# A routed feed-forward on one core: the first expert in plain float32, and the second stage's gating moved from VectorE to ScalarE and GpSimd

## The chip, the core and the metric

The kernel runs on one core of a Trainium2 chip. A core has engines that work side by side, each through its own instructions in order: TensorE (PE in the profile; its weight loads are PEld), VectorE (DVE), ScalarE (ACT), GpSimd (POOL) and SyncE (SP), which here issues transfers. They share an on-chip memory (SBUF); TensorE writes to PSUM. An instruction that needs another engine's result waits at the head of its engine's queue, and all behind it wait too. The metric is the time of one execution on the device in microseconds.

## What is computed

Attention gives 2304 tokens of 512 numbers. Each of 8 experts takes 288 of them, by a greedy choice over all scores in falling order, and sends them through its own two-matrix network. A second, common network with a gate follows. Cut to what matters:

```python
# expert e, for its 288 tokens (mask)
h = np.maximum(x[mask] @ w1[e], 0.0)      # 512 -> 1024
out[mask] = h @ w2[e]                     # 1024 -> 512
# second network, for all tokens
h = x @ w_in                              # 512 -> 2048
relu6 = np.clip(h + 3.0, 0.0, 6.0)
g = h * relu6 / 6.0
return g @ w_out                          # 2048 -> 512
```

## The kernel before

After attention (to about 300 us of the trace) the work goes by **slots**, one an expert, in the order in which experts fill up. A slot holds one expert's 288 tokens, transposed, and has 24 **steps**: 8 of the first stage (`kind` 0, the expert's network, 128 hidden units a step) and 16 of the second (`kind` 1, the gated network). A step is `l1` (4 blocks of 128 into the hidden units `h`, a PSUM tile with 2 buffers), the activation `ev` (for `kind` 1 the gating), and `l2` (into 4 accumulators `acc`). `l2` of a step is issued after `l1` of two steps later (`LAG = 2`), so that the activation has that long.

The matmuls are in a rounded float32 format, fp32r. To keep precision every operand is split into a high part (a rounded copy, `xh`, `yh`, `gh`, the first half of `w`) and a low part (the difference, `xl`, `yl`, `gl`), and each product is made of three: high by high, high by low, low by high (L1118 to L1120 in `mm3`, L1187 to L1190 in `l1`). A step has 24 matmuls of 288 columns. Weights are split by `split_w` (L1106 on ScalarE, L1108 the low part, on GpSimd; in slot 0 every sixth on VectorE). The second network's weights are the same for all slots: they are split once in slot 0, half are kept in `WB`, half written to DRAM (`hl`) and read back later. A helper, `Convert`, makes those weights from bits on VectorE (L978 to L981) and a sign multiply on GpSimd (L988), partly within slot 0 (`cv.rest`).

The second stage's gating is: ScalarE `t` = relu(h + 3) (L1204), ScalarE `pc` = h (L1205), VectorE `t` = min(t, 6) x pc (L1206), ScalarE `gh` = t/6 (L1207), VectorE `gl` = t/6 - gh (L1208).

The **router** runs beside this: phase s + 1 finds, during slot s, the next expert's tokens. Its parts, in order: take out the tokens chosen (`close`, `best`), turn the keys (`rx`, `rw`: matmuls of TensorE; copies `ks` by ScalarE; from phase 2 on through DRAM, `kd`, into `rHw` and `rLw`), then a **search** for the 288th largest key: 4 rounds over high digits (`rHw`) and 4 over low (`rLw`). A round counts, in each of 128 partitions, which of 2304 keys reach that partition's threshold. Of the columns VectorE counts 1440 (L714) and ScalarE 864 with a Sign that sums (L716); L717 merges both into `cnt`; a transpose (L722) and a comparison (`fl`, L725) give the next thresholds. Then come `rhs` (a matmul to all partitions, `rp<-rhs`), small VectorE operations, `tot` (three tiny matmuls), positions, `roc`, 20 `ua` matmuls, and `ids`, by which GpSimd gathers the tokens (`xg`). They are transposed on TensorE and split (`x_in`: L1138 and L1139 on ScalarE, L1140 `xl` on VectorE) in the last steps of the slot.

What runs where in an engine's queue comes from the order in which the code is written, then a scheduler's: the router is a generator, and `step()` takes its next unit when a counter (`hold`) that falls by `RATE` a half step reaches zero; every `yield n` puts n onto it, in the search `SLACK` a round.

```python
def step():
    hold[0] -= RATE[s > 0]
    while hold[0] <= 0:
        hold[0] += next(units, 1e9)
```

Of the kernel before, what the change touches and what calls it, by code (L numbers as in the profile page):

```python
# [514 lines left out]
class Router:  # L515
# [288 lines left out]
    def phase(self, s):  # L804
# [6 lines left out]
        if s < E - 1:  # L811
# [13 lines left out]
            half = SHARE  # L825
# [187 lines left out]
def experts(ctx, tc, rt, x_dram, cv, w1, w2, out, ident, cap, B, S):  # L1013
# [52 lines left out]
    def load(s, j):  # L1066

        if j >= FA + FB * (s == 0):
            return
        if j >= FA:  # L1070
            f = j - FA
            raw = raws[s, 1, f] = wp.tile([128, 1024], F32, name="raw", tag="raw", bufs=RAW)
            if f < cv.pre // 2:
                nc.sync.dma_start(raw, cv.wb[:, f])
            else:
                conv.extend([lambda u=u: cv.rest(raw[:, u * 512:(u + 1) * 512], 2 * f + u) for u in range(2)])
# [13 lines left out]
    cnt = [0]  # L1090

    def split_w(i, part):
# [273 lines left out]
```

## Time and profile before

| | |
|---|---|
| median of 3 runs | 1131.04 us (1130.54 to 1137.7) |
| the profiled execution | 1130.45 us, its span in the trace 1128.6 us |
| TensorE busy | 961.0 us (85%), mean granted clock 0.926 |
| VectorE, ScalarE, GpSimd busy | 727.9, 605.6, 435.8 us (64, 54, 39%) |
| slot 0 starts, ends | 346.7, 466.2 us |
| slots 1 to 7 end | 567.8, 668.4, 767.5, 866.6, 959.3, 1038.7, 1128.6 us |

Slot boundaries are the first `l1` matmul of a slot in the trace. The shares of busy time are means over stages with different limits, so what follows is read by slot. A line of a timeline gives start, duration, engine, source line, operation, the tiles written and read, and in brackets how long its engine had been idle before and who released it. The granted clock is a share of TensorE's full speed (1.00 is 2.4 GHz, 0.50 is 1.2 GHz).

### The profile page before, as it was taken

What the parts mean: (1) busy time and instruction counts of PE and PEld (TensorE: products, weight loads), DVE (VectorE), ACT (ScalarE), POOL (GpSimd) and SP (SyncE); (2) the same over time, 40 slices, a digit from 0 to 9 for tenths busy, and PEclk for the clock granted to TensorE, in tenths of its full rate; (3) what the DMA queues carried; (4) which work ended last, traced back from release to release, by engine and by line L of the source; (5) the groups of instructions that cost most, each with busy time, mean ns of one, the idle gap of its engine ahead of it and who ended that gap; (6) DMA issues with size and microseconds to landing.
All of it is one profiled execution on the core that took longest, in us unless ns stands there. A gap on an engine that the chain in (4) does not pass through costs nothing.

```text
span 1128.6 us, 20123 instructions
## 1 busy us (share of the span) xinstructions
PE 961.0 (85%) x6748; PEld 885.6 (78%) x6748; DVE 727.9 (64%) x1933; ACT 605.6 (54%) x1499; POOL 435.8 (39%) x346
## 2 busy tenths in 40 slices
PE   4888888898317788789889889899989999999997
PEld 3676766675217688779789788889978999999996
DVE  7888897986773996783973856586385534234332
ACT  5786776875334764534653563455256235445442
POOL 7657556661424664331250044026104402603400
PEclk9999999998657997889999999899899899999999
DMA  7889879887133865349229525823752562572540
GB/s 172 240 239 258 232 205 266 206 228 202 43 99 112 297 214 163 96 146 270 84 73 286 138 75 195 222 82 119 232 148 68 183 202 90 182 243 73 181 159 21
DMA packets 122999, 190.28 MB, mean 169 GB/s; under 512 B 21904, under 2 KB 72464, under 8 KB 122896
## 3 DMA queue, kind: packets, MB, share of 16 engines
q1 hardware_dynamic: 119136, 179.54, 53.2%
q0 software_dynamic: 3072, 9.44, 2.8%
q8 instruction: 54, 0.88, 0.3%
q14 instruction: 49, 0.40, 0.1%
q10 hardware_dynamic: 688, 0.02, 0.0%
HBM read 144.60 MB, written 25.61 MB: 151 GB/s over the span
## 4 chain that ended last, share of the span: by engine, by line
PE 34%; DVE 20%; issue 8%; DMA 5%; ACT 1%; POOL 1%; POOLq 0%; DVEq 0%; ACTq 0%; SPq 0%
DVE rcmp L714 5%; PE h L1187 5%; PE acc L1119 5%; PE h L1188 5%; PE acc L1120 5%; PE h L1190 5%; PE acc L1118 5%; DMA rHw<-kd 4%; PE rp L701 2%; DVE gl L1201 2%; DVE gl L1208 2%; DVE cnt L717 1%; DVE t L1206 1%; DVE fl L725 1%; POOL w L1108 1%
## 5 line engine op out<-in xcount | busy, mean ns | idle before, releaser
L1108 POOL TENSOR_TENSOR w<-raw,w 128x512 fp32r<-128x512 f32 x135 | 180.6, 1352 | 383.5 <-ACT w L1106 291.4
L1119 PE MATMUL acc<-gl,w 128*128 128x288 f32 x512 | 156.7, 312 | 19.3 <-DVE gl L1208 13.0
L1120 PE MATMUL acc<-gh,w 128*128 128x288 f32 x512 | 153.4, 306 | 0.0
L1118 PE MATMUL acc<-gh,w 128*128 128x288 f32 x512 | 139.9, 310 | 13.7 <-ACT gh L1207 13.5
L1206 DVE SCALAR_TENSOR_TENSOR t<-t,pc 128x288 f32<-128x288 f32 x128 | 61.4, 480 | 117.4 <-ACT pc L1205 117.2
L1119 PEld LDWEIGHTS acc<-gl,w 128*128 128x128 f32 x512 | 101.8, 199 | 24.3 <-DVE gl L1208 16.7
L1204 ACT ACTIVATE t<-h,rthree 128x288 f32<-128x288 f32 x128 | 63.5, 496 | 102.8 <-PE h L1190 97.5
L1118 PEld LDWEIGHTS acc<-gh,w 128*128 128x128 f32 x512 | 93.9, 197 | 16.3 <-ACT gh L1207 16.2
L1106 ACT ACTIVATE w<-raw 128x512 fp32r<-128x512 f32 x144 | 89.6, 633 | 28.5 <-PE acc L1120 16.3
L282 ACT ACTIVATE P<-P,mx 128x128 f32<-128x128 f32 (+2 forms) x144 | 83.6, 581 | 37.1 <-DVE mx L267 35.7
L1120 PEld LDWEIGHTS acc<-gh,w 128*128 128x128 f32 x512 | 101.8, 199 | 0.0
L1201 DVE TENSOR_TENSOR gl<-t,gh 128x288 fp32r<-128x288 f32 x64 | 52.7, 824 | 73.6 <-ACT gh L1200 73.6
L1207 ACT ACTIVATE gh<-t 128x288 fp32r<-128x288 f32 x128 | 56.6, 444 | 64.4 <-DVE t L1206 64.4
L1208 DVE SCALAR_TENSOR_TENSOR gl<-t,gh 128x288 fp32r<-128x288 f32 x128 | 66.1, 517 | 29.8 <-ACT gh L1207 28.0
L1187 PE MATMUL h<-yh,w 128*128 128x288 f32 x256 | 74.4, 309 | 6.6 <-ACT pc L1205 6.6
L1119 PE MATMUL acc<-gl,WB 128*128 128x288 f32 x256 | 75.9, 303 | 2.7 <-DVE gl L1208 2.6
L246 PE MATMUL sc<-kh,qs 128*128 128x128 f32 (+3 forms) x128 | 49.7, 399 | 30.9 <-DVE qs L218 12.2
L1187 PE MATMUL h<-xh,w 128*128 128x288 f32 x256 | 75.3, 313 | 0.3 <-ACT gh L1200 0.3
L1120 PE MATMUL acc<-gh,WB 128*128 128x288 f32 x256 | 74.8, 298 | 0.0
L1188 PE MATMUL h<-xh,w 128*128 128x288 f32 x256 | 74.4, 310 | 0.0
L1188 PE MATMUL h<-yh,w 128*128 128x288 f32 x256 | 72.5, 301 | 0.0
L1187 PE MATMUL h<-yh,WB 128*128 128x288 f32 x256 | 71.1, 298 | 0.0
(294 smaller groups left out, 2806.8 us busy)
## 6 DMA issues: line engine op xcount, KB each, us to landing
w<-hl SPq DMA_DIRECT2D x112, 512.0 KB, 5.0
raw<-in_moe_w_dram SPq DMA_DIRECT2D x128, 256.0 KB, 4.3
kh<-knh SPq DMA_DIRECT2D x60, 144.0 KB, 2.6
raw<-in_moe_w_in_dram SPq DMA_DIRECT2D x16, 512.0 KB, 4.0
raw<-in_moe_w_out_dram SPq DMA_DIRECT2D x16, 512.0 KB, 4.6
hl<-w SPq DMA_DIRECT2D x16, 512.0 KB, 6.2
wb<-wf SPq DMA_DIRECT2D x28, 256.0 KB, 2.9
raw<-wb SPq DMA_DIRECT2D x14, 512.0 KB, 5.0
```

The source lines that it names most:

```text
L282: nc.scalar.activation(x[:, :w], x[:, :w], AF.Exp, bias=mx, scale=-1.0, accum_out=col)
L1106: nc.scalar.activation(hi, src, AF.Copy)
L1108: j = (nc.vector if v else nc.gpsimd).tensor_tensor(lo, src, hi.bitcast(F32), op=OP.subtract)
L1118: nc.tensor.matmul(p, ah, bh, start=first, stop=False)
L1119: nc.tensor.matmul(p, ah, bl, start=False, stop=False)
L1120: rt.behind = nc.tensor.matmul(p, al, bh, start=False, stop=last)
L1187: nc.tensor.matmul(p, wk[k][0], x[k][0], start=(k == 0), stop=False)
L1188: nc.tensor.matmul(p, wk[k][1], x[k][0], start=False, stop=False)
L1201: nc.vector.tensor_tensor(gl, t, gh.bitcast(F32), op=OP.subtract)
L1204: nc.scalar.activation(t, p, AF.Relu, bias=rt.three)
L1206: nc.vector.scalar_tensor_tensor(t, t, 6.0, pc, op0=OP.min, op1=OP.mult)
L1208: nc.vector.scalar_tensor_tensor(gl, t, 1.0 / 6.0, gh.bitcast(F32), op0=OP.mult, op1=OP.subtract)
```

## The change

Four edits. (1) **Slot 0 in plain float32**: `l1_whole` and the first branch of `l2` multiply unsplit tokens, hidden units and weights, 4 matmuls each in place of 12, on raw weight tiles (two of 512 columns, 4 buffers each). x and y are copied once, by ScalarE and VectorE in turn; the gate is two ScalarE operations and one of VectorE. The second network's weights are still split in slot 0, for later slots, after their step, all low parts on GpSimd. (2) **Gating of slots 1 to 7**: VectorE's two operations go; ScalarE takes a second relu (6 - relu(3 - h), so that t ends as relu6), GpSimd the product and the low part. The first stage's `gl` and y's low part stay on VectorE. (3) **The low part of x** goes to GpSimd. (4) **The search from phase 1 on** counts all 2304 columns on VectorE; Sign and merge go; the constants that set the pace change with it.

```diff
-SLACK = 2.6
+SLACK = 2.3
@@ search
-            below = wk.tile([128, 1], F32, name="below", bufs=2)
-            nc.scalar.activation(cmp[:, n:].bitcast(BF), W[:, n:], AF.Sign, bias=T, scale=-1.0, accum_out=below)
-            nc.vector.scalar_tensor_tensor(cnt, below, -0.5, cnt, op0=OP.mult, op1=OP.add)
+            if shared:
+                below = wk.tile([128, 1], F32, name="below", bufs=2)
+                nc.scalar.activation(cmp[:, n:].bitcast(BF), W[:, n:], AF.Sign, bias=T, scale=-1.0, accum_out=below)
+                nc.vector.scalar_tensor_tensor(cnt, below, -0.5, cnt, op0=OP.mult, op1=OP.add)
@@ phase (and in it yield 1 -> 2, yield 3 -> 5; in route, 3 -> 4)
-            half = SHARE
+            half = SHARE if s == 0 else 0
@@ experts
-    EVERY, FIRST = 6, 6
-    RATE = 1.4, 0.9
+    RATE = 1.5, 0.95
@@ split_w
-        v = s == 0 and (cnt[0] % EVERY == 0 or cnt[0] <= FIRST)
-        j = (nc.vector if v else nc.gpsimd).tensor_tensor(lo, src, hi.bitcast(F32), op=OP.subtract)
-        if s == 0 and kind == 0:
-            after(tc, j, rt.last if v else rt.fetch)
+        nc.gpsimd.tensor_tensor(lo, src, hi.bitcast(F32), op=OP.subtract)
@@ x_in
+            if s == 0:
+                x = whole("x", f"x{c}", 1)
+                if c % 2:
+                    nc.vector.tensor_copy(x, p[:, :cap])
+                else:
+                    nc.scalar.activation(x, p[:, :cap], AF.Copy)
+                XT[s].append(x)
+                continue
...
-            nc.vector.tensor_tensor(hl[1], t, hl[0].bitcast(F32), op=OP.subtract)
+            nc.gpsimd.tensor_tensor(hl[1], t, hl[0].bitcast(F32), op=OP.subtract)
@@ new
+    def l1_whole(kind, f, x, w, prev=None):
+        p = ps.tile([128, 512], F32, name="h", tag="h", bufs=2)[:, :cap]
+        for k in range(KC):
+            rt.behind = nc.tensor.matmul(p, w[:, k * 128:(k + 1) * 128], x[k], start=(k == 0), stop=(k == KC - 1))
...
+                nc.scalar.activation(t, p, AF.Relu, bias=rt.three)
+                nc.scalar.activation(pc, p, AF.Copy, scale=1.0 / 6.0)
+                nc.vector.scalar_tensor_tensor(g, t, 6.0, pc, op0=OP.min, op1=OP.mult)
@@ l1
-                nc.scalar.activation(t, p, AF.Relu, bias=rt.three)
-                nc.scalar.activation(pc, p, AF.Copy)
-                nc.vector.scalar_tensor_tensor(t, t, 6.0, pc, op0=OP.min, op1=OP.mult)
-                nc.scalar.activation(gh, t, AF.Copy, scale=1.0 / 6.0)
-                nc.vector.scalar_tensor_tensor(gl, t, 1.0 / 6.0, gh.bitcast(F32), op0=OP.mult, op1=OP.subtract)
+                nc.scalar.activation(t, p, AF.Relu, bias=rt.three, scale=-1.0)
+                nc.scalar.activation(pc, p, AF.Copy, scale=1.0 / 6.0)
+                nc.scalar.activation(t, t, AF.Relu, bias=rt.six, scale=-1.0)
+                nc.gpsimd.tensor_tensor(t, t, pc, op=OP.mult)
+                nc.scalar.activation(gh, t, AF.Copy)
+                nc.gpsimd.tensor_tensor(gl, t, gh.bitcast(F32), op=OP.subtract)
@@ l2
+            if not isinstance(g, tuple):
+                rt.behind = nc.tensor.matmul(p[:, :cap], w[:, o * 128:(o + 1) * 128], g, start=first, stop=last)
+                continue
@@ main loop
+        if s == 0:
+            for u in range(2 * kind):
+                split_w(i, u)
+            load(i + RAW)
```

The change moves line numbers: L714, L721, L722, L725 of before are L715, L723, L724, L727 of the changed kernel, L1108 is L1106, L1187 to L1190 are L1221 to L1224, L1118 to L1120 are L1114 to L1116, L701 is L702.

TensorE's order around phase 2's `rhs` matmul (`rp<-rhs`; `h` is of `l1`, `acc` of `l2`). Before, some six steps into slot 1:

```order
L1187 MATMUL h<-xh,w_5880 128x288
L1188 MATMUL h<-xh,w_5880 128x288
L1190 MATMUL h<-xl,w_5880 128x288 x4
L1118 MATMUL acc_5803<-gh,w_5838 128x288
L1119 MATMUL acc_5803<-gl,w_5838 128x288
L1120 MATMUL acc_5803<-gh,w_5838 128x288
L701 MATMUL rp<-rhs,ronef 128x16
L1159 MATMUL ot<-ident,yo 96x128 x4
L1118 MATMUL acc_5804<-gh,w_5838 128x288
```

After, behind the first steps' `l1` of slot 1 and the last `l2` of slot 0 (`g,raw`), ahead of slot 1's first `l2`, two steps into it:

```order
L1222 MATMUL h<-xh,w_5135 128x288
L1224 MATMUL h<-xl,w_5135 128x288 x4
L1251 MATMUL acc_4564<-g,raw_4948 128x288
L1251 MATMUL acc_4565<-g,raw_4948 128x288
L1251 MATMUL acc_4566<-g,raw_4948 128x288
L1251 MATMUL acc_4567<-g,raw_4948 128x288
L1165 MATMUL ot<-ident,yo 96x128
L702 MATMUL rp<-rhs,ronef 128x16
L1114 MATMUL acc_5309<-gh,w_5016 128x288
L1115 MATMUL acc_5309<-gl,w_5016 128x288
L1116 MATMUL acc_5309<-gh,w_5016 128x288
```

It stands about four steps earlier in slot 1.

VectorE's order within phase 2's search. Before, two high rounds, with gating (L1206, L1208), `xl` and merge between:

```order
L714 TENSOR_SCALAR rcmp,cnt<-rHw,T 128x1440
L721 TENSOR_SCALAR rG<-T,rcz 128x1
L1140 TENSOR_TENSOR xl<-t,xh 128x288
L717 SCALAR_TENSOR_TENSOR cnt<-below,cnt 128x1
L722 STREAM_TRANSPOSE rrowH<-cnt 128x32
L725 SCALAR_TENSOR_TENSOR fl,T<-rrowH,rG 128x33
L1208 SCALAR_TENSOR_TENSOR gl<-t,gh 128x288
L714 TENSOR_SCALAR rcmp,cnt<-rHw,T 128x1440
```

After, the last low round and what follows to `rhs`, with a gate of slot 0 (L1212) and a block of weight conversion (L981 to L984) between:

```order
L715 TENSOR_SCALAR rcmp,cnt<-rLw,T 128x2304
L723 TENSOR_SCALAR rG<-T,rcz 128x1
L981 TENSOR_SCALAR raw_4948<-raw 128x512
L724 STREAM_TRANSPOSE rrowL<-cnt 128x32
L1212 SCALAR_TENSOR_TENSOR g<-t,pc 128x288
L982 SCALAR_TENSOR_TENSOR raw_4948<-raw,raw_4948 128x512
L983 TENSOR_SCALAR raw<-raw 128x512
L727 SCALAR_TENSOR_TENSOR fl,T<-rrowL,rrem,rG 128x33
L984 TENSOR_SCALAR raw_4948<-raw 128x512
L854 TENSOR_SCALAR rhs<-rsel,T 128x8
```

The counts are wider, the merges gone, and the gates of slot 0's last steps stand behind counts.

GpSimd's order in a slot's last steps, after (a stretch of slot 1; `w` splits of the next slot's weights, `t` and `gl` the gating, `xl` of the next tokens):

```order
L1242 TENSOR_TENSOR t<-t,pc 128x288
L1106 TENSOR_TENSOR w_7318<-raw_7291,w_7318 128x512
L1244 TENSOR_TENSOR gl<-t,gh 128x288
L1242 TENSOR_TENSOR t<-t,pc 128x288
L1106 TENSOR_TENSOR w_7419<-raw_7303,w_7419 128x512
L1244 TENSOR_TENSOR gl<-t,gh 128x288
L1242 TENSOR_TENSOR t<-t,pc 128x288
L1106 TENSOR_TENSOR w_7422<-raw_7304,w_7422 128x512
L1146 TENSOR_TENSOR xl<-t,xh 128x288
L1244 TENSOR_TENSOR gl<-t,gh 128x288
```

Before, only the `w` splits stood there. In the last six steps of a slot they are 8 splits, 12 gating operations and 4 `xl`.

## Rows read from the trace of the kernel before

**Rows 1.** Slots 0, 2, 4, 5, 6: us, PE, PEld, DVE, ACT, POOL busy, clock, DMA
```profile
core 0 of [0], span 1128.6 us
...
346.70:466.20 119.50, 97.78 (x630) 91.75 (x630) 92.17 (x191) 72.37 (x163) 63.03 (x47) 0.87 0.59 192
...
567.80:668.40 100.60, 89.17 (x635) 86.16 (x634) 64.24 (x154) 48.91 (x118) 26.37 (x22) 0.97 0.52 153
...
767.50:866.60 99.10, 90.53 (x635) 87.07 (x634) 62.57 (x154) 48.22 (x116) 26.61 (x22) 0.95 0.49 153
866.60:959.30 92.70, 90.44 (x649) 90.11 (x649) 39.97 (x102) 39.35 (x97) 27.34 (x22) 0.94 0.46 149
959.30:1038.70 79.40, 79.04 (x603) 78.78 (x602) 28.32 (x53) 39.26 (x97) 26.92 (x22) 1.00 0.53 175
```

**Rows 2.** TensorE's waits in slots 1 to 4: total us, times, longest us
```profile
PE acc L1119 <- DVE gl L1208: 10.5, 13, 2.3
PE acc L1118 <- ACT gh L1207: 8.4, 8, 2.4
PE h L1187 <- ACT pc L1205: 5.9, 4, 2.9
PE rp L701 <- DVE tot L885: 4.4, 2, 2.7
```

**Rows 3.** ScalarE's timeline in phase 3's search: start, duration, work, idle before
```profile
535.44 1.02 ACT L716 ACTIVATE rcmp<-rHw,T 128x864 bf16<-128x864 uint16 x1 [0.94 <-DVE fl L725]
...
536.79 0.48 ACT L1204 ACTIVATE t<-h,rthree 128x288 f32<-128x288 f32 x1
```

**Rows 4.** VectorE's groups by form, whole kernel: busy us, mean ns, idle before
```profile
L1208 DVE SCALAR_TENSOR_TENSOR gl<-t,gh 128x288 fp32r<-128x288 f32 x128 | 66.1, 517 | 29.8 <-ACT gh L1207 28.0 <-PE acc L1120 0.5 <-issue 0.2
...
L978 DVE TENSOR_SCALAR raw<-raw 128x512 int32<-128x512 int32 x4 | 3.5, 889 | 0.0
```

**Rows 5.** VectorE, 457.7 to 494.5 us (busy, mean ns | idle); counts (min/median/max)
```profile
L717 DVE SCALAR_TENSOR_TENSOR cnt<-below,cnt 128x1 f32<-128x1 f32 x8 | 8.4, 1056 | 0.0
...
L1201 DVE TENSOR_TENSOR gl<-t,gh 128x288 fp32r<-128x288 f32 x6 | 2.7, 445 | 0.0
...
L714 DVE TENSOR_SCALAR_CACHE_REDUCE rcmp<-rHw,T x21: 1703/1709/1715, 296.4 to 831.2; 128x1440 uint16<-128x1440 uint16 x21
```

**Rows 6.** Phase 2: timelines of ScalarE, VectorE; router's matmuls (min/median/max, starts)
```profile
446.90 0.70 ACT L757 ACTIVATE ks<-rw 64x288 uint16<-64x288 f32 x2 [1.16 <-PE rw L701]
...
457.71 1.71 DVE L714 TENSOR_SCALAR_CACHE_REDUCE rcmp<-rHw,rT 128x1440 uint16<-128x1440 uint16 x1 [4.62 <-DMA rHw<-kd]
...
L701 PE MATMUL rp<-ua,roc x20: 209/311/312, 508.6 to 511.8; 128*96 128x6 bf16 x20
...
L701 PE MATMUL rp<-rhs,ronef x2: 366/370/374, 494.5 to 494.7; 128*128 128x16 f32 x2
```

**Rows 7.** Subtractions on GpSimd and VectorE by line; TensorE's timeline at a float32 matmul
```profile
L1108 POOL TENSOR_TENSOR w<-raw,w x135: 1252/1295/2658, 339.8 to 1057.9; 128x512 fp32r<-128x512 f32 x135
...
L1108 DVE TENSOR_TENSOR w<-raw,w x9: 678/679/1279, 332.3 to 419.2; 128x512 fp32r<-128x512 f32 x9
...
L204 POOL TENSOR_TENSOR qnl<-qn,qnh x15: 1405/1436/1951, 20.5 to 239.7; 128x576 fp32r<-128x576 f32 x15
...
69.75 0.66 PE L374 MATMUL mem<-MZ,qp 128*128 128x146 f32 x4
70.25 0.96 PE L393 MATMUL zl<-wg,oT 128*128 128x16 f32 x8
```

**Rows 8.** A merge behind a run of GpSimd; all merges' min/median/max
```profile
480.38 5.05 POOL L1108 TENSOR_TENSOR w<-raw,w 128x512 fp32r<-128x512 f32 x4
...
481.05 4.40 DVE L717 SCALAR_TENSOR_TENSOR cnt<-below,cnt 128x1 f32<-128x1 f32 x1
...
L717 DVE SCALAR_TENSOR_TENSOR cnt<-below,cnt x56: 143/159/4404, 294.2 to 848.5; 128x1 f32<-128x1 f32 x56
```

**Rows 9.** Window behind the `ua` products of slot 2, columns as rows 1
```profile
599.10:602.40 3.30, 3.30 (x15) 3.30 (x16) 0.48 (x3) 0.00 (x0) 1.65 (x2) 0.50 1.03 401
```

More of the change, by code (lines that the diff above doesn't have):

```diff
@@ L635, in consts @@
         nc.vector.memset(t("three", [128, 1]), 3.0)
+        nc.vector.memset(t("six", [128, 1]), 6.0)
         t("keyi", [128, NT, E], I32)
@@ L1064, in gather, with load @@
             rt.fetch = i
-    def load(s, j):
-        if j >= FA + FB * (s == 0):
+    def load(j):
+        s, kind, f = order[j]
+        if s and kind:
             return
[L1070 to L1076, printed above, removed]
+        raw = raws[j] = [wp.tile([128, 512], F32, name=f"raw{u}", tag=f"raw{u}", bufs=RAW) for u in range(2)]
+        if kind:
+            for u in range(2):
+                if f < cv.pre // 2:
+                    nc.sync.dma_start(raw[u], cv.wb[:, f, u * 512:(u + 1) * 512])
+                else:
+                    conv.append(lambda u=u: cv.rest(raw[u], 2 * f + u))
             return
-        f = j
         if f == 0:
@@ L1098, in split_w @@
         hi, lo = w[:, :512], w[:, 512:]
-        W[i, part] = hi, lo
+        if s:
+            W[i, part] = hi, lo
         if kind and s:
@@ L1120, in mm3, with whole @@
         rt.behind = nc.tensor.matmul(p, al, bh, start=False, stop=last)
+    def whole(name, tag, bufs):
+        return act.tile([128, cap], F32, name=name, tag=tag + "h", bufs=bufs)
     def parts(name, tag, bufs):
@@ L1171, in out_units, with y_in @@
         return ev, [tr(a) for a in range(3)]
-    def y_in(acc):
+    def y_in(s, acc):
         y = []
         for o, p in enumerate(acc):
+            if s == 0:
+                y.append(whole("y", f"y{o}", 1))
+                if o % 2:
+                    nc.vector.tensor_copy(y[o], p[:, :cap])
+                else:
+                    nc.scalar.activation(y[o], p[:, :cap], AF.Copy)
+                continue
             hl = parts("y", f"y{o}", 1)
@@ L1180, in y_in, with ev @@
         return y
+    def l1_whole(kind, f, x, w, prev=None):
+        p = ps.tile([128, 512], F32, name="h", tag="h", bufs=2)[:, :cap]
+        for k in range(KC):
+            rt.behind = nc.tensor.matmul(p, w[:, k * 128:(k + 1) * 128], x[k], start=(k == 0), stop=(k == KC - 1))
+            if prev is not None:
+                after(tc, rt.behind, prev)
+                prev = None
+        def ev():
+            g = whole("g", "g", LAG + 2)
+            if kind == 0:
+                nc.scalar.activation(g, p, AF.Relu)
+            else:
+                t = act.tile([128, cap], F32, name="t", tag="t", bufs=2)
+                pc = act.tile([128, cap], F32, name="pc", tag="pc", bufs=2)
+                nc.scalar.activation(t, p, AF.Relu, bias=rt.three)
+                nc.scalar.activation(pc, p, AF.Copy, scale=1.0 / 6.0)
+                nc.vector.scalar_tensor_tensor(g, t, 6.0, pc, op0=OP.min, op1=OP.mult)
+            return g
+        return ev
     def l1(kind, f, x, w, prev=None):
@@ L1224, in ahead @@
             while nw[part] < min(i + 2 * SPLIT[0], len(order)):
-                held = [j for j in range(i - part * LAG, nw[part] + 1) if j >= 0 and not (order[j][1] and order[j][2] % 2)]
-                if len(held) > SPLIT[part] or order[nw[part]][0] not in reg or order[nw[part]][:1] + (0, 0) not in raws:
+                held = [j for j in range(max(i - part * LAG, FA + FB), nw[part] + 1)
+                        if not (order[j][1] and order[j][2] % 2)]
+                if len(held) > SPLIT[part] or nw[part] not in raws and not order[nw[part]][1]:
                     break
@@ L1264, in experts @@
             routed(s + 1)
-            for u in range(RAW):
-                load(s + 1, u)
+            for u in range(RAW if s else 0):
+                load(pos[s + 1, 0, u])
             xs = x_in(s + 1)
@@ L1278, in experts @@
             conv.pop(0)()
-        e = l1(kind, f, X[s, 1] if kind else XT[s], W.pop((i, 0)), rt.behind if kind and f == 1 else None)
+        e = (l1 if s else l1_whole)(kind, f, X[s, 1] if kind else XT[s], W.pop((i, 0)) if s else raws[i][0],
+                                    rt.behind if kind and f == 1 else None)
         step()
```

44 lines of the change are left out of this document (21 added, 23 removed).

## The prediction

> **What bounds the kernel now.** I read the windows by slot first [rows 1]. Slot 6, in which no router runs, takes 79.4 us with TensorE busy for 79.0 of them at full clock: that is the floor of 24 steps, 79.4/24 = 3.31 us a step. Slots 2 to 4 have the same matmuls and take 99.1 to 100.6 us, so 20 us a slot stand above the floor (slot 3 takes 99.1 like slot 4). TensorE's waits from slot 1 to slot 4 [rows 2] say where: for VectorE's `gl` and ScalarE's `gh` of the second stage's gating, for the `pc` copy that frees a PSUM buffer, and for the router's small results. The four rows printed are 29 us, 7 a slot, and I count 9 with the view's smaller ones. The rest is the router's own matmuls (20 `ua` products, 508.6 to 511.8, a start-to-end of 3.45 us [rows 6], and about 1.1 us of others) and low clock: the mean granted clock of slot 4 is 0.95, and at half clock half of the time is lost, so 0.05 x 99 = 5 us. One such stretch stands right behind the `ua` products of one slot: 3.3 us at a granted clock of 0.50 [rows 9], the lower of the two levels (1.2 GHz), worth 1.7 us.
>
> Why the gating is late is in ScalarE's timeline [rows 3]: a Sign count of the search waits 0.94 us for VectorE's `fl`, then runs 1.02 us, and everything behind it in ScalarE's order (`t`, `pc`, `gh`) waits as well (the next `t` starts at 536.79). Search and gating hold each other up.
>
> **The change, part by part.** *Search on VectorE alone (phases 1 to 7).* A count of 1440 columns takes 1.71 us and hardly varies [rows 5]. 2304 columns are between 1.71 (if columns cost nothing) and 1.71 x 1.6 = 2.74; I take 2.6 start to start, since the start-up does not grow: +0.9 a round, 8 rounds, **+7.2 us** of VectorE. The merge `cnt<-below` goes: 8.4 us in the search of phase 2 [rows 5], 1.3 of work (8 x the median 0.159 [rows 8]) and 7.1 of standing behind GpSimd: one merge took 4.40 us while a run of four GpSimd subtractions, 5.05 us, was on [rows 8].
>
> *Gating of slots 1 to 7.* VectorE loses two operations a step (`gl` 0.517 us mean [rows 4], `t` like it), 16 us a slot. ScalarE gets one more activation of 0.4 to 0.5 (0.48 in [rows 3]) and loses the Signs, about 1.2 us each with the read of the sum, 8 a phase; its four gating operations are 1.8 us of a 3.3 us step, so it stays free. GpSimd gets two products of 128x288 a step. No such shape is in the trace on that engine. Its nearest rows are 128x512 at 1.295 us and 128x576 at 1.436 [rows 7]: in proportion 0.73, on the line through both 1.295 - 224 x 0.141/64 = 0.80, and 1.295 if size did not matter. I take 0.77, nearest to the two scalings. The chain from the last `h` matmul to `gl` is then 0.5 + 0.4 + 0.5 + 0.77 + 0.44 + 0.77 = 3.4 us against about 2.3; with LAG = 2 the second matmuls have two steps, 6.6 us, so this is hidden, and only the kernel's end pays it: +1 us.
>
> *Low parts of x on GpSimd.* In the last six steps of slots 1 to 6 GpSimd holds, by the order, 8 weight splits, 12 gating operations and 4 `xl`: 8 x 1.295 + 16 x 0.77 = 22.7 us against 6 x 3.31 = 19.9. It falls some 2.8 us behind; the LAG takes part of it and I charge **2 us** a slot. Without the cover of the LAG it is 2.8.
>
> The Trainium skill, "GPSIMD Engine Reference", section 4.1 (engine selection), says that two-input elementwise work belongs on VectorE and is about twice slower on GpSimd. The trace agrees at 128x512 (1.295 against 0.68 us on VectorE, its fastest [rows 7]). By it an estimate for 128x288 is 2 x 0.46 = 0.92 us, which is a rival below.
>
> *Slot 0 in float32.* A float32 matmul is two TensorE instructions: `mem<-MZ,qp` is issued as two matmuls and the trace has four instructions of 146 columns in 0.50 us, from 69.75 to 70.25 [rows 7]. So 0.25 us for a matmul of 146 columns, 0.25 x 288/146 = 0.49 for 288, and 8 a step: **3.88 us** in place of 3.31, if it scales by columns; 0.25 (no scaling, 2.0 a step) is the other end. That adds 13.7 us to 24 steps of TensorE and takes the splits, the gating's `gl` and the subtractions from VectorE, whose counts, gating and weight splits filled slot 0 before: 92 of 119.5 us busy [rows 1].
>
> The next slot's search decides where this ends. Its low-digit matmuls `rw` stand at step 16.4 of slot 0 after (20.4 before). 16.4 x 3.88 = 63.6; + 4.0 for `ua` and other router matmuls; + 5.0 for three low-clock stretches of 1.65; + 6.3 of waits (VectorE's copies of y stand in the order between counts: about 4; the router's matmuls 2.3; estimates): 346.7 + 78.9 = 425.6. From `ks` to the first count 10.8 us passed [rows 6]; with up to 2 more for the transfer, 12: the search starts at 437.6, in place of 457.7. It took 36.8 us (457.7 to the `rhs` matmul at 494.5 [rows 6]). Now: +7.2 counts, -8.4 merges, -7.1 (16 gating, x-split and copy operations of 0.445 each stood among them), +8.0 for what stands there now (two conversion blocks of four operations, the dearest 0.889 [rows 4], 5.8 in all, and five `g` of 0.45), and +10.7 for standing behind GpSimd: the 7.1 that the merges bore falls on `fl`, `g` and the conversion's combining operations, half as much again since GpSimd now has all of slot 0's splits. 36.8 + 7.2 - 8.4 - 7.1 + 8.0 + 10.7 = 47.2, so `rhs` is ready at 484.8. In TensorE's order it stands at step 2 of slot 1 now, 6.1 before; TensorE is there at 346.7 + 24 x 3.88 + 15.3 + 2 x 3.31 = 462 and waits some 22 us. What is late next is all of slot 1 behind it.
>
> The Trainium skill, "SBUF - State Buffer", section "Who interferes with whom", says that a VectorE operation with two SBUF inputs and a GpSimd operation that reads SBUF exclude each other, whoever issues first holding the ports for its whole instruction. The trace agrees that there is waiting, but the 4.40 us [rows 8] are longer than one GpSimd instruction of 1.3. By one instruction a merge at most, the 10.7 would be 8 x 1.3 = 10.4: no other sum.
>
> **Sum.** Slot 1 from there: 22 x 3.31 = 72.8, `ua` 3.45, others 1.1, low clock 2 x 1.7, GpSimd 2, residual waits 2.5: 85.3, so slot 2 starts at 570.1 (567.8 before). Slots 2 to 4: 79.4 + 3.45 + 1.1 + 1.7 + 2 + 2.5 = 90.2 each (100.6, 99.1, 99.1): 840.7. I let the clock's other dips go with the waits; if they stay it is 3 x 3.3 = 10 us more. Slot 5, with two `ua` groups: 79.4 + 6.9 + 1.5 + 3.4 + 2 + 1 = 94.2 (92.7): 934.9. Slot 6: 81.4 (79.4): 1016.3. Slot 7, from 1038.7 to the end 89.9, becomes 90.9: a span of 1107.2, 21.4 less than the 1128.6 of the profiled execution, which took 1130.45 us itself, 0.6 under the median of 1131.04. With the same 1.85 outside the span: **1109 us**. Slots 0 and 1 lose 2, slots 2 to 4 win 28, the rest loses 5.
>
> **Rivals.** *A. The larger gain.* No standing behind GpSimd in phase 2 (-10.7), no GpSimd backlog (-2 x 6): 1109 - 22.7 = 1086. For it: the merge that stood longest is gone, and counts never slowed (1.70 to 1.715 us [rows 5]). Against: `fl` also has two inputs.
> *B. GpSimd paces (the slower side).* If the product of 128x288 costs c, the last six steps of six slots cost 16 x (c - 0.77) x 6 more. At 1.295 that is 50: 1159. It decides from c = 1.12 (over 1142). For it: that engine's rows are 1.3 and more for anything so far. Against: 1.295 to 1.436 does grow with size.
> *C. The page's factor of two, c = 0.92:* +14, 1123, within 1%.
> *D. The search becomes the path in every slot.* `rw` to `rhs` is 16 to 17 steps before and 14 to 14.5 after: 14.5 x 3.31 = 48 us must hold transfer and search. 12 + 8 rounds x 3.3 + 3 = 41 leaves 7; if `fl` and the middle operations stand behind whole GpSimd runs as `cnt` did (4.40), TensorE waits some 4 to 5 us at `rhs` in five phases: +22, 1131.
>
> **How the numbers follow.** The forecast has a chance of 0.46 (own range 1096 to 1119), A 0.18, B 0.10, C 0.08, D 0.18. A measurement of this kernel tells about 1% from no change. Faster by over 1% (under 1120): 0.46 + 0.18 = 0.64; within 1%: C and D, 0.26; slower: B, 0.10. The range leaves out B and the far half of A: 1085 to 1136.
>
> **What would show it.** Right: Sign and merge rows gone in slots 1 to 5, counts of 2.6 us, GpSimd products of 0.77, TensorE's waits for `gl` and `gh` near nothing in slots 2 to 4, slots of 90 us, and one wait of about 22 us at `rhs` early in slot 1. Wrong: waits for GpSimd's `t` or `gl` of several us at the end of each slot (B, C), waits of 4 us and more at `rhs` in slots 1 to 5 (D), slot 0's matmuls not 0.49 us per product, or a search in slot 0 that ends before TensorE gets to it (A).

## The result

The changed kernel takes 1117.38 us (median of 4 runs, 1113.8 to 1122.37) against 1134.37 of the kernel before on the same chip: a ratio of 0.9871 (0.9831 to 0.9910). A second measurement beside the last experiments gave 0.9853 (0.9806 to 0.9901). The forecast was 1109 in a range of 1085 to 1136. The profiled execution took 1115.67 us, its span is 1113.9; the forecast span was 1107.2.

The windows of the changed kernel by slot, 0 to 7 (columns as in [rows 1]: the stretch, its length, busy us and instructions of PE, PEld, DVE, ACT, POOL, granted clock, share of the DMA engines, GB/s):

```profile
339.20:466.10 126.90, 111.66 (x437) 83.91 (x437) 86.68 (x172) 46.34 (x100) 54.70 (x43) 0.89 0.57 178
466.10:569.20 103.10, 94.74 (x630) 91.18 (x630) 63.49 (x120) 49.18 (x119) 60.59 (x63) 0.90 0.56 165
569.20:657.80 88.60, 85.34 (x636) 83.44 (x635) 56.60 (x115) 47.30 (x115) 56.57 (x59) 1.00 0.58 171
657.80:753.90 96.10, 88.73 (x634) 86.37 (x633) 58.76 (x121) 47.33 (x115) 56.23 (x59) 0.96 0.55 155
753.90:848.60 94.70, 88.97 (x634) 86.51 (x633) 54.96 (x110) 47.12 (x115) 55.59 (x59) 0.96 0.55 162
848.60:941.00 92.40, 90.37 (x649) 88.93 (x648) 17.36 (x45) 46.07 (x112) 55.01 (x59) 0.96 0.46 150
941.00:1023.60 82.60, 80.07 (x601) 78.99 (x601) 8.97 (x16) 45.78 (x112) 54.42 (x59) 1.00 0.52 168
1023.60:1113.90 90.30, 81.59 (x614) 80.51 (x612) 14.42 (x18) 42.82 (x103) 45.76 (x51) 0.96 0.34 113
```

| | before | after | forecast |
|---|---|---|---|
| slot 0 starts | 346.7 | 339.2 | 346.7 |
| slot 0 | 119.5 | 126.9 | 108 |
| slot 1 | 101.6 | 103.1 | 115 |
| slots 2, 3, 4 | 100.6, 99.1, 99.1 | 88.6, 96.1, 94.7 | 90.2 each |
| slot 5 | 92.7 | 92.4 | 94.2 |
| slot 6 | 79.4 | 82.6 | 81.4 |
| slot 7 | 89.9 | 90.3 | 90.9 |

So the span is 14.7 us shorter: 7.5 at the start of slot 0, 19 in slots 2 to 4, and about 12 given back in slots 0, 1 and 6. TensorE's waits in the changed kernel (total us, times, longest), first over all slots, then in slots 2 to 4 alone:

```profile
PE h L1221 <- DMA w<-hl: 9.1, 2, 5.3
PE acc L1115 <- POOL gl L1244: 9.0, 12, 1.4
PE acc L1251 <- DVE g L1212: 8.3, 3, 3.9
PE h L1198 <- DVE y L1185: 5.6, 2, 4.9
PE h L1221 <- ACT xh L1145: 2.8, 1, 2.8
```

```profile
PE h L1221 <- DMA w<-hl: 9.1, 2, 5.3
PE acc L1115 <- POOL gl L1244: 4.5, 6, 1.4
PE acc L1114 <- DVE yo L1156: 1.7, 2, 1.5
PE h L1221 <- ACT pc L1240: 0.7, 2, 0.4
```

In the kernel before, the longest of the list in slots 2 to 4 were these:

```profile
PE acc L1118 <- ACT gh L1207: 8.0, 7, 2.4
PE acc L1119 <- DVE gl L1208: 6.4, 7, 2.3
```

So of the waits of [rows 2] those for `gh` and `tot` are gone in slots 2 to 4, those for `pc` fell from 5.4 to 0.7 us, and those for `gl` went from 6.4 us for VectorE to 4.5 for GpSimd. New ones stand there for the reloads of the second network's weights (`w<-hl`), in slots 3 and 4, and in slot 0 for VectorE's `g` and `y`.

### The profile page after: what moved, and what is told of

Read it like the earlier page. It is cut to its first block, busy times and chain, and to the rows that moved or that the text cites. A ratio compares the mean times of both kernels' runs of the same rounds, so it can differ in the third digit from the quotient of the medians.

```text
span 1113.9 us, 19553 instructions
## 1 busy us (share of the span) xinstructions
PE 972.9 (87%) x6556; PEld 876.5 (79%) x6556; DVE 637.6 (57%) x1587; ACT 587.8 (53%) x1471; POOL 625.4 (56%) x595
## 4 chain that ended last, share of the span: by engine, by line
PE 56%; DVE 15%; DMA 10%; POOL 7%; issue 5%; ACT 4%; SPq 2%; POOLq 0%; DVEq 0%; ACTq 0%
PE h L1221 7%; PE h L1222 6%; PE h L1224 6%; PE acc L1115 6%; PE acc L1116 6%; PE acc L1114 6%; PE h L1198 3%; DMA w<-hl 3%; PE acc L1251 3%; PE rp L702 3%; DVE rcmp L715 2%; PE av L328 2%; POOL gl L1244 2%; POOL t L1242 2%; PE sc L246 1%
## 5 line engine op out<-in xcount | busy, mean ns | idle before, releaser
L1106 POOL TENSOR_TENSOR w<-raw,w 128x512 fp32r<-128x512 f32 x128 | 168.1, 1325 | 108.4 <-ACT w L1105 107.8
L1242 POOL TENSOR_TENSOR t<-t,pc 128x288 f32<-128x288 f32 x112 | 92.0, 823 | 110.6 <-ACT t L1241 110.6
L1115 PE MATMUL acc<-gl,w 128*128 128x288 f32 x448 | 131.8, 304 | 9.0 <-POOL gl L1244 9.0
L1116 PE MATMUL acc<-gh,w 128*128 128x288 f32 x448 | 130.0, 300 | 0.0
L1114 PE MATMUL acc<-gh,w 128*128 128x288 f32 x448 | 114.8, 310 | 1.7 <-DVE yo L1156 1.7
L1244 POOL TENSOR_TENSOR gl<-t,gh 128x288 fp32r<-128x288 f32 x112 | 91.1, 819 | 30.7 <-ACT gh L1243 30.7
L1115 PEld LDWEIGHTS acc<-gl,w 128*128 128x128 f32 x448 | 86.6, 193 | 12.1 <-POOL gl L1244 11.8
L1116 PEld LDWEIGHTS acc<-gh,w 128*128 128x128 f32 x448 | 86.5, 193 | 0.0
L1114 PEld LDWEIGHTS acc<-gh,w 128*128 128x128 f32 x448 | 79.0, 196 | 3.4 <-DVE yo L1156 2.4
L1221 PE MATMUL h<-yh,w 128*128 128x288 f32 x224 | 64.1, 305 | 11.4 <-DMA w<-hl 9.1
L991 POOL TENSOR_TENSOR wf<-wa,wf 128x512 f32<-128x512 f32 x28 | 37.7, 1347 | 62.0 <-DVE cm L380 14.6
L1221 PE MATMUL h<-xh,w 128*128 128x288 f32 x224 | 67.5, 320 | 3.5 <-ACT xh L1145 2.8
L267 DVE CUSTOM_DVE_ANT_0 P<-sc,mask 128x128 f32<-128x128 f32 (+3 forms) x128 | 59.4, 479 | 12.8 <-PE sc L247 8.8
L1222 PE MATMUL h<-xh,w 128*128 128x288 f32 x224 | 65.8, 313 | 0.0
L1116 PE MATMUL acc<-gh,WB 128*128 128x288 f32 x224 | 63.9, 295 | 0.0
```

The source lines that it names most:

```text
L1106: nc.gpsimd.tensor_tensor(lo, src, hi.bitcast(F32), op=OP.subtract)
L1114: nc.tensor.matmul(p, ah, bh, start=first, stop=False)
L1115: nc.tensor.matmul(p, ah, bl, start=False, stop=False)
L1221: nc.tensor.matmul(p, wk[k][0], x[k][0], start=(k == 0), stop=False)
L1222: nc.tensor.matmul(p, wk[k][1], x[k][0], start=False, stop=False)
L1242: nc.gpsimd.tensor_tensor(t, t, pc, op=OP.mult)
```

## Experiments

Each kernel is compared with the kernel before on the same chip. The attention part varies by some us between executions (the first `rhs` matmul stands between 321.5 and 328.3 us in these profiles), so single profiles are read by slot, not by their end.

**Each half of the change without the other.**

> The changed kernel with one part undone: the gating of slots 1 to 7 again has VectorE's two operations (min times pc, low part); all else stays. Theory: counts of 2.6 us stand ahead of two gating operations a step on VectorE, the chain of 2.3 us grows by up to 5.2 and passes the two steps (6.6 us) that it has, so TensorE waits for gl and gh again: slots 2 to 4 take 93 to 98 us in place of 88.5, 96.2 and 94.7, the whole some 1125 us. Rival: taking Sign and merge away was the gain by itself, the gating can stay on VectorE: within 3 us of the changed kernel, about 1116.

```diff
-                nc.gpsimd.tensor_tensor(t, t, pc, op=OP.mult)
-                nc.gpsimd.tensor_tensor(gl, t, gh.bitcast(F32), op=OP.subtract)
+                nc.vector.scalar_tensor_tensor(t, t, 6.0, pc, op0=OP.min, op1=OP.mult)
+                nc.vector.scalar_tensor_tensor(gl, t, 1.0 / 6.0, gh.bitcast(F32), op0=OP.mult, op1=OP.subtract)
```

> The changed kernel with one part undone: the search of phases 1 to 7 again shares its columns with ScalarE (Sign, merge); the gating stays on ScalarE and GpSimd. Theory: a Sign that waits for VectorE's thresholds holds four gating operations of ScalarE behind it, and merges stand behind GpSimd, which now works in every step: slots 2 to 4 at 93 to 97 us, the whole some 1125 us. Rival: the Signs were never the hold, a shorter search frees VectorE: 1110 us or less.

```diff
-            half = SHARE if s == 0 else 0
+            half = SHARE
```

Measured: 1141.59 us, ratio 1.0065 (1.0033 to 1.0096), and 1153.4 us, 1.015 (1.0097 to 1.0204). Each half alone is slower than the kernel before; only together do they gain. Both keep the other edits, the pace among them. Slots 2 to 4 take 100.5, 100.2 and 97.0 us with the gating on VectorE, 102.1, 98.4 and 102.9 with the shared search: 297.7 and 303.4 us together, against 298.8 in the kernel before and 279.4 in the changed one. The windows of gate_back, slots 2 to 4:

```profile
581.20:681.70 100.50, 89.42 (x636) 86.64 (x635) 66.35 (x153) 39.42 (x99) 31.28 (x27) 0.95 0.52 151
681.70:781.90 100.20, 89.69 (x635) 86.97 (x634) 66.77 (x149) 39.55 (x99) 29.86 (x26) 0.95 0.52 151
781.90:878.90 97.00, 89.46 (x634) 87.15 (x633) 63.64 (x140) 39.86 (x100) 30.09 (x26) 0.95 0.50 155
```

There the gain is gone. What makes the halves slower than the kernel before lies mostly in slots 0 and 1, which take 238.8 and 240.6 us together, against 221.1 before and 230.0 in the changed kernel.

The rivals fall, and both numbers are worse than the theory's 1125. It thought of counts and Signs that stand ahead of the gating. A larger hold in these runs is the *first* count of a search. It waits at the head of its engine's queue for the transfer of the digits, and the gating stands behind it. VectorE's timeline with the gating back, then its waits for that transfer from 575 to 960 us in the kernel before and in the changed one, and TensorE's longest wait in gate_back:

```profile
635.47 2.61 DVE L715 TENSOR_SCALAR_CACHE_REDUCE rcmp<-rHw,rT 128x2304 uint16<-128x2304 uint16 x1 [9.09 <-DMA rHw<-kd]
```

```profile
DVE rcmp L714 <- DMA rHw<-kd: 21.7, 3, 8.2
```

```profile
DVE rcmp L715 <- DMA rHw<-kd: 39.9, 3, 17.4
```

```profile
642.25 1.33 PE L1114 MATMUL acc<-gh,w 128*128 128x288 f32 x4 [7.05 <-ACT gh L1242]
```

VectorE stands 9.09 us until 635.47, the gating's `t` stands behind that count and the next, and TensorE waits 7.05 us until 642.25 for the `gh` that comes of it. No run separates the wait for the digits from the two counts. At the first counts in slots 2 to 4 TensorE waits 7.1, 5.1 and 5.3 us, 17.5 of the 29.0 that the view lists there. The changed kernel's VectorE waits longer for the same transfer, up to 17.4 us, but nothing that TensorE needs in those steps stands behind it. With the Sign back, the same happens on ScalarE (its timeline):

```profile
823.88 0.50 ACT L1239 ACTIVATE t<-h,rthree 128x288 f32<-128x288 f32 x1
830.54 1.01 ACT L718 ACTIVATE rcmp<-rHw,rT 128x864 bf16<-128x864 uint16 x1 [6.16 <-DMA rHw<-kd]
831.46 0.19 ACT L718 ACTIVATION_READ_ACCUMULATOR rcmp<-rHw,rT 128x1 f32 x1
831.56 0.52 ACT L1241 ACTIVATE t<-t,rsix 128x288 f32<-128x288 f32 x1
831.98 0.38 ACT L1240 ACTIVATE pc<-h 128x288 f32<-128x288 f32 x1
```

`t` began at 823.88, its next step waits behind the Sign until 831.56, and the `pc` that frees the PSUM buffer ends at 832.4: TensorE's waits for `pc` in slots 1 to 5 are 18.5 us, the longest 6.5. In the kernel before, both engines stood there for the same transfer in every phase from the second on, ScalarE 23.2 us in phases 4 to 6. But the longest waits of TensorE beside those three counts are short, 7.5 of the 27.4 us that the view lists in slots 2 to 4:

```profile
626.95 0.40 PE L1118 MATMUL acc<-gh,w 128*128 128x288 f32 x1 [2.43 <-ACT gh L1207]
724.47 0.40 PE L1187 MATMUL h<-yh,w 128*128 128x288 f32 x1 [2.17 <-ACT pc L1205]
824.45 0.61 PE L1187 MATMUL h<-yh,w 128*128 128x288 f32 x1 [2.86 <-ACT pc L1205]
```

**Slot 0.**

> The changed kernel with slot 0 as before: split operands, 24 matmuls a step, gating on VectorE, part of the weight splits on VectorE; the other three edits and the pace stay, from slot 1 on. Theory: slot 0 starts at 346.7 again, since VectorE's weight splits hold up GpSimd's first gather, and VectorE bounds it as before; float32 in slot 0 costs TensorE 14 us and saves about as much in waits: slot 2 starts at 565 to 570, the whole 1110 to 1117 us, no clear difference. Rival: float32 is the main gain, without it the whole is over 1125.

The edit is the kernel before with the diff's parts of `search`, `phase` and the pace, and for `s > 0` alone those of `x_in` and of the gating:

```diff
-            nc.vector.tensor_tensor(hl[1], t, hl[0].bitcast(F32), op=OP.subtract)
+            (nc.gpsimd if s else nc.vector).tensor_tensor(hl[1], t, hl[0].bitcast(F32), op=OP.subtract)
```

Measured: 1119.06 us, 0.9843 (0.9793 to 0.9893). That cannot be told from the changed kernel: float32 in slot 0 brings nothing measurable. Slot 0 starts 14.7 us after the token numbers `ids` are ready, as before (14.8), and 7.7 in the changed kernel.

> The kernel before with one number changed: the first six weight splits no longer go to VectorE (they go to GpSimd like the others). Theory: VectorE's run of subtractions with two inputs from 332.3 us on held GpSimd's first gather (4.95 us in place of 1.3); without it slot 0 starts some 5 to 7 us sooner, at 340 to 342, and the end moves by 2 to 6 us since VectorE bounds slot 0. Rival: the gather's length has nothing to do with VectorE: slot 0 starts at 346 to 347.

```diff
-    EVERY, FIRST = 6, 6
+    EVERY, FIRST = 6, 0
```

Measured: 1127.71 us, 0.9952 (0.9921 to 0.9983): faster by the 2 to 6 us expected, but not for the reason given. The gather is short, as expected, and slot 0 still starts 14.9 us after `ids`. (`EVERY` leaves the sixth split on VectorE.) GpSimd's and VectorE's timelines at the first gather: before (GpSimd, VectorE), then the changed kernel (GpSimd), then this run (GpSimd, VectorE):

```profile
332.41 4.95 POOL L1061 DMA_INDIRECT xg<-x_dram,ids  x1 [23.49 <-DVE rleft L914]
333.84 2.48 DVE L1108 TENSOR_TENSOR w<-raw,w 128x512 fp32r<-128x512 f32 x4
```

```profile
331.99 1.34 POOL L1063 DMA_INDIRECT xg<-x_dram,ids  x1 [23.49 <-DVE rleft L917]
```

```profile
338.76 7.35 POOL L1108 TENSOR_TENSOR w<-raw,w 128x512 fp32r<-128x512 f32 x6
338.69 7.46 DVE L687 TENSOR_TENSOR rm<-rm,rdead 128x20 f32<-128x20 f32 x1
```

Before, a run of VectorE's subtractions stretched the gather from 1.34 to 4.95 us. With those subtractions on GpSimd, a run of six of them held a VectorE operation of 128x20 for 7.46 us. That one feeds the router's `rx`, which stands ahead of the token transposes in TensorE's order. In these rows each of the two engines stands while the other subtracts. The changed kernel's slot 0 splits nothing at that moment, so it meets neither case. What no_first gained lies elsewhere in slots 0 to 4, one profile does not say where.

**The low part of the next tokens.**

> The changed kernel with the low part of the next tokens on VectorE again (GpSimd has 4 operations of 0.82 us a slot less). Theory: GpSimd's backlog in the last six steps, charged at 2 us a slot, shrinks by 3.3 us: waits for GpSimd's gl (1.3 to 1.6 us a slot) go, slot 6 at 80 to 81 us in place of 82.7; the whole 1108 to 1114. Rival: GpSimd has slack enough and counts of 2.6 us hold the low parts: slots 2 to 4 as long or longer, the whole 1115 to 1122.

```diff
-            nc.gpsimd.tensor_tensor(hl[1], t, hl[0].bitcast(F32), op=OP.subtract)
+            nc.vector.tensor_tensor(hl[1], t, hl[0].bitcast(F32), op=OP.subtract)
```

Measured: 1125.87 us, 0.9933 (0.9903 to 0.9963): some 7 to 9 us slower than the changed kernel by the ratios (0.9871 and 0.9853 there), and 9 above pace_back and rhw_act below, which ran beside it. Slot 6 gains 1.1 us (81.5), as the theory had it, but the rival's side weighs more, by another road: `x_in` and the gating share the two buffers of `t` on ScalarE. TensorE's waits from 470 to 960 us, then ScalarE's, here, then ScalarE's in the changed kernel:

```profile
PE h L1221 <- ACT pc L1240: 14.9, 9, 5.8
```

```profile
ACT t L1239 <- DVE xl L1146: 13.1, 5, 5.9
```

```profile
ACT t L1239 <- POOL xl L1146: 9.3, 10, 1.6
```

A count ahead of `xl` on VectorE keeps the buffer, the gating's first step waits up to 5.9 us, and TensorE for `pc`.

**The reload waits.**

> The changed kernel with the numbers of the pace (SLACK, RATE, three yields) as before; by the order the low-digit matmuls of the next phase stand at steps 9.5 and 9.3 of slots 3 and 4 in place of 7.5 and 6. Theory: the waits for reloaded second-stage weights in slots 3 and 4 (5.3 and 3.7 us) come from the router's transfer in front of those loads; later transfers leave them alone: no such wait, slots 3 and 4 at 89 to 91 us, the whole 1107 to 1113. Rival: the loads are late because TensorE is now faster than they are, wherever the transfer stands: the waits stay, 1116 or more.

```diff
-SLACK = 2.3
+SLACK = 2.6
-    RATE = 1.5, 0.95
+    RATE = 1.4, 0.9
```

> The changed kernel with the two transfers of digits to all partitions (rHw, rLw) issued by ScalarE in place of SyncE, so that the reloads of weights do not queue behind them. Theory: it is the queue: waits for the reloads in slots 3 and 4 under 1 us, but ScalarE stands some 2 to 4 us a phase for the write of the digits, which the two steps of slack take; the whole 1108 to 1116. Rival: it is the bandwidth that both share: reload waits within 1.5 us of 5.3 and 3.7.

```diff
-            nc.sync.dma_start(W.rearrange("p b s -> p (b s)"), bass.AP(
+            nc.scalar.dma_start(W.rearrange("p b s -> p (b s)"), bass.AP(
```

Measured: 1117.1 us, 0.9853 (0.9819 to 0.9887), and 1117.24, 0.9881 (0.9822 to 0.9940): no difference from the changed kernel, and not the gain that either theory had. So the pace by itself is no part of the change's gain. With the pace of before the reload waits are gone from the list, slots 3 and 4 take 92.8 and 90.5 us, slot 2 takes 93.0, and other waits have come (TensorE, 470 to 960 us):

```profile
PE rp L702 <- DVE tot L888: 8.2, 4, 3.1
PE acc L1115 <- POOL gl L1244: 7.8, 10, 1.4
PE acc L1115 <- DVE gl L1235: 4.5, 2, 3.9
```

With the transfer on ScalarE's queue one reload wait of 5.1 us stays, in slot 4 (98.3 us there), and slot 3 has none (88.9). When the transfer comes decides on the waits; whether it acts by the queue or by the bandwidth stays open, since in rhw_act one of two went.

**VectorE out of slot 0's way.**

> The changed kernel with slot 0's four copies of y all on ScalarE (half of them stood behind VectorE's counts). Theory: the clock falls behind a wait: without the 4.9 us wait at the start of slot 0's second stage the 10.2 us of low clock that cover it go too, slot 0 is 8 to 10 us shorter up to there, and as nothing else of slot 0 is bound by it part of it stays: the whole 1109 to 1115. Rival: the low clock falls anyway and ScalarE's copies are as late: within 2 us of 1117.

```diff
-                if o % 2:
-                    nc.vector.tensor_copy(y[o], p[:, :cap])
-                else:
-                    nc.scalar.activation(y[o], p[:, :cap], AF.Copy)
+                nc.scalar.activation(y[o], p[:, :cap], AF.Copy)
```

Measured: 1114.69 us, 0.9851 (0.9795 to 0.9907), not to be told from the changed kernel beside it (0.9853). The wait of 4.9 us became 2.8, and the low clock behind it shrank from one stretch of 10.2 us to one of 3.4. The stretch in the changed kernel with the wait in it (windows, timeline), then the low one in y_act:

```profile
376.90:387.10 10.20, 6.72 (x13) 4.37 (x14) 10.02 (x23) 3.01 (x7) 3.71 (x3) 0.50 0.26 87
```

```profile
379.65 2.29 PE L1198 MATMUL h<-y,raw 128*128 128x288 f32 x4 [4.87 <-DVE y L1185]
```

```profile
380.80:384.20 3.40, 3.32 (x7) 2.42 (x8) 3.33 (x8) 2.16 (x6) 3.40 (x3) 0.50 0.04 4
```

What was won there went into waits for conversion at the end of slot 0 (5.3 us for `raw`, 4.2 for `pc`), where the next search and the last conversion blocks stand: slot 0 takes 130.8 us in this profile.

> The changed kernel with slot 0's gate product on GpSimd (as in the later slots) and all copies of y on ScalarE, so that VectorE's counts hold nothing of TensorE's in slot 0. Theory: the waits for g and y (8.3 and 5.6 us) and part of the 14 us of low clock behind them go: slot 0 takes 110 to 116 us in place of 126.9; TensorE then waits for rhs early in slot 1 some 5 us, the whole 1104 to 1112. Rival: GpSimd, with all weight splits of slot 0, becomes the hold: slot 0 over 122 us, no gain.

```diff
-                nc.vector.scalar_tensor_tensor(g, t, 6.0, pc, op0=OP.min, op1=OP.mult)
+                nc.scalar.activation(t, t, AF.Relu, bias=rt.six, scale=-1.0)
+                nc.gpsimd.tensor_tensor(g, t, pc, op=OP.mult)
```

(and the edit of y_act.) Measured: 1115.35 us, 0.9847 (0.9816 to 0.9878). Slot 0 takes 125.8 us, as the rival had it, and not 110 to 116. The waits for `g` fall to 3.1 us, and in their place stands this one:

```profile
PE h L1195 <- POOL raw L991: 8.4, 1, 8.4
```

> As slot0_off (slot 0's gate product on GpSimd, y on ScalarE), and in slot 0 the conversion's sign multiply on VectorE in place of GpSimd, where weight splits stood ahead of it (8.4 us of TensorE's wait). Theory: with that wait gone slot 0 takes 113 to 118 us, the next search is the last hold, the whole 1104 to 1111. Rival: the conversion is then held behind VectorE's counts by as much: the whole 1112 or more.

```diff
-        self.sign(w, w, i)
+        self.sign(w, w, i, self.nc.vector)
```

> As slot0_off2 with the numbers of the pace as before (no wait for weight reloads in slots 3 and 4 in that run, but 8 us for tot). Theory: in slots 1 to 4 pace only moves waits between the router's results and the weight reloads: within 4 us of slot0_off2. Rival: the reload waits are worth their 9 us: that much less than slot0_off2.

(slot0_off2 with the edit of pace_back; after_again is the changed kernel.)

> The changed kernel itself once more beside these, on the same chip, as what y_act, slot0_off2 and slot0_off3 are to be compared with: 0.983 to 0.991 of the kernel before, 1113 to 1122 us.

Measured, on one chip: slot0_off2 1109.43 us (1106.29 to 1112.84), 0.979 (0.9749 to 0.9832); slot0_off3 1118.57, 0.9862 (0.9821 to 0.9903); the changed kernel 1116.5 (1112.67 to 1122.05), 0.9853. slot0_off2 is the fastest version, some 7 us below the changed kernel beside it. Its slot 0 takes 126.4 us all the same, not the 113 to 118 expected: near its end TensorE waits 7.0 us, put down to a ScalarE weight split. Against the changed kernel's profile its gain lies in slots 1 and 3 (98.6 and 91.7 us), where the theory did not look for it; why slot 1 is shorter stays open. slot0_off3 shows that the pace counts here: with that of before the waits for `tot` (9.2) and `gl` (5.2) are back. It is 9 us slower than slot0_off2, where the theory had at most 4 and the rival had it faster.

## Why the prediction was right, and where its sum was off

The direction, the mechanism in slots 2 to 4 and the range held; the size was 2.0% forecast and 1.3% measured (1.5 in the second comparison). By its steps:

- *Search on VectorE alone, gating off it.* Right: 2.6 us a count was measured as 2.61, and of the waits of [rows 2] nearly all but those for `gl`, now GpSimd's, went. But the reason was a part of it. The prediction put the hold down to Sign, `fl` and counts, and in the kernel before that may well be the larger share, since the waits at the first counts are 7.5 of 27.4 us there. In gate_back and sign_back a search's first operation, which waits for the digits, goes with the largest part (17.5 of 29.0 us, and 15.8 of 28.6 in slots 2 to 4). In the changed kernel the engine that waits for the router's transfer, up to 17.4 us, is one whose queue TensorE does not wait for at that place.
- *Slots 2 to 4 at 90.2.* Slot 2 took 88.6 with no low clock at all, so the other dips of the clock did go with the waits, and even the one behind `ua` that was charged did not come there. Slots 3 and 4 took 96.1 and 94.7: the term that was too small is the residual of 2.5 us, which did not price what the change moves on SP's queue. The faster pace puts the digits' transfers in front of the first weight reloads: 5.3 and 3.7 us, and a low stretch of 3.4 us behind each wait.
- *Products of 128x288 on GpSimd at 0.77.* They take 0.806 (median), 0.82 in the mean, near the line through both sizes (0.80). Rivals B and C, 1.12 and 0.92, fall by this row. The Trainium skill, "GPSIMD Engine Reference", section 4.1, is near: twice slower is 1.8 times here (0.806 against VectorE's 0.458 for the same shape). The last six steps hold 8 x 1.3 + 16 x 0.82 = 23.5 us against 19.9; slot 6 is 3.2 us longer, where 2 was charged.

```profile
L1242 POOL TENSOR_TENSOR t<-t,pc x112: 795/806/1916, 520.1 to 1100.4; 128x288 f32<-128x288 f32 x112
```

- *Slot 0 in float32.* The matmul's price was right: two starts of 0.243 us at full clock, 0.49. The sum of the slot was not: 108 forecast, 126.9 measured. Of the 18.5 too much, waits make 9: TensorE is idle 15.2 us of the slot (`g` 8.3, `y` 5.6, `pc` 1.2), where 6.3 stood. Low clock makes some 6: five stretches at or near 0.50 hold 21.35 us of busy time, of which half, 10.7, is lost, where 5 stood. The other 4 are the router's matmuls and the token transposes, 111.66 - 10.7 - 93.1 = 7.9 us, where 4.0 stood. The sum of the windows 339.2 to 342.6, 376.9 to 387.1, 414.3 to 417.6, 445.2 to 451.9 and 458.9 to 462.2:

```profile
sum 26.90, PE 21.35 PEld 14.85 DVE 21.70 ACT 7.62 POOL 13.44; mean PE 4.27 PEld 2.97 DVE 4.34 ACT 1.52 POOL 2.69
```

  The `g` that the order shows behind VectorE's counts was counted as VectorE's time and not as TensorE's wait.
- *`rhs` ready at 484.8, TensorE waiting 22 us.* Wrong. The search ran from 433.8 to 472.2, 38.4 us in place of 47.2, and TensorE came to `rhs` at 480.8, later than the result. The term that failed is 10.7 us for standing behind GpSimd. VectorE's groups from 433.7 to 472.3 show about 4: `g` 0.664 in place of 0.45, two operations of 128x8 at 1.2 in place of 0.23, and less in `fl` and the conversion.

```profile
L1212 DVE SCALAR_TENSOR_TENSOR g<-t,pc 128x288 f32<-128x288 f32 x5 | 3.3, 664 | 0.0
...
L850 DVE TENSOR_SCALAR rhs<-rsel,T 128x8 f32<-128x8 f32 x1 | 1.2, 1239 | 0.0
```

  GpSimd worked back to back there too, eight operations from 458.25 to 467.40 us, but an `fl` in the middle of them took 0.83 us in place of 0.25 and ended with one of them (GpSimd, VectorE):

```profile
458.25 1.50 POOL L991 TENSOR_TENSOR raw<-wa,raw 128x512 f32<-128x512 f32 x1 [2.46 <-DVE fl L727]
459.70 2.50 POOL L1106 TENSOR_TENSOR w<-raw,w 128x512 fp32r<-128x512 f32 x2
462.16 0.79 POOL L1146 TENSOR_TENSOR xl<-t,xh 128x288 fp32r<-128x288 f32 x1
461.43 0.83 DVE L727 SCALAR_TENSOR_TENSOR fl<-rrowL,rrem,rG 128x33 f32<-128x33 f32 x1
```

  Why VectorE stood so briefly here and 4.40 us in [rows 8] stays open. The start of slot 2 came out right (569.2 for 570.1) by luck, because four errors met: slot 0 started 7.5 us sooner, which was not foreseen, it lasted 18.5 longer, the wait at `rhs`, 23 by the sum, was not there, and the rest of slot 1 took 11 longer. Some 6 of these 11 are low clock: at 0.90 it costs some 9 us of the 94.74 that TensorE is busy, where 3.4 stood.
- *Rivals A and D.* D did not come: TensorE waited for `rhs` in no phase, since the search in slots 1 to 4 had room. Of A, the shorter search in phase 2 came, and with it its sign, a search that ends before TensorE gets to `rhs`; the backlog of GpSimd did not vanish.
- *Low part of x on GpSimd.* It was charged as a loss of 2 us a slot. xl_back shows a gain of some 7 to 9 us in all, since VectorE's counts would have kept the shared buffer.
- *Float32 as a part of the change.* The forecast let slots 0 and 1 lose 2 us; they lost 9 in the profile and won 7.5 at the gather. slot0_split agrees: no measurable difference.

## What to carry to other kernels

Ask of each engine's queue what stands at its head waiting for a transfer, and whose work stands behind it: a long, slow search is harmless on an engine that the matmuls do not wait for, and harmful in small shares on two that they do. Take such a change whole, or test its halves: here either half alone loses 0.7 to 1.5%, both win 1.3%. A number read from a row where two engines collide (here 7.1 us of merges, 10.7 with the addition) is not a fixed price: beside GpSimd's work in the changed kernel the same search paid about 4.

## What the runs showed of the hardware

The first GpSimd gather took 1.16 to 1.34 us in every profile in which VectorE did not split weights beside it, and 4.95 in the two in which it did (before and slot0_split); the other way round a run of six GpSimd subtractions (7.35 us) held a VectorE operation of 128x20 for 7.46. In these rows the wait lasts over a whole run of instructions; the `fl` of 0.83 us above, within a run of eight, stood for one at most. The Trainium skill, "SBUF - State Buffer", section "Who interferes with whom", tells of such a lock for one instruction's length; that row agrees with it, and the first ones are several times that.

TensorE's granted clock was 1.00 over all of slot 2 (88.6 us), in which it waited some 3 us in all, and fell to 0.50 (1.2 GHz) around waits of 2.8 to 5.3 us in the other slots up to 4, around two of 1.1 and 1.4 close together in slot 1, and behind the `ua` products of slots 0, 1, 3 and 4, though not behind those of slot 2; a shorter wait (2.8 for 4.9 us) came with a shorter low stretch (3.4 for 10.2). In slot 0 the three low stretches around waits hold 14.7 us of busy time, so by half of it they cost some 7 us on top of the 15.2 waited.
